# Gated linear attention followed by a gated state-space projection: weights loaded and converted by quarter, and the opening of the schedule put in another order

## The chip, the cores and the metric

The kernel runs on one core of one Trainium2 chip. The metric is device time in microseconds (us) of one execution; the number that counts is the median of several runs. Everything is float32 on the chip; the inputs q, k, v and alpha come as float32, the two weight matrices as float64, which the kernel converts itself.

## The reference, cut to what matters

```python
# q, k, v, alpha: (4 batches, 8 heads, 768 steps, 48)
for t in range(768):
    state = alpha[t][:, None] * state + outer(k[t], v[t])   # 48 x 48 for each batch and head
    y[t] = q[t] @ state
x = y with the heads side by side                            # (4, 768, 384)
val, gate = split(x @ w_in)                                  # w_in 384 x 1024, 512 each
for t in range(768):
    h = exp(A_log) * h + val[t]
    ys[t] = h
out = (silu(gate) * ys) @ w_out                              # w_out 512 x 384
```

## The kernel before, in words

**Blocks.** A block is 256 steps of one batch, so there are N = 12 blocks, three to a batch. Block m is worked in two halves. The attention half makes xT (the 384 features by 256 steps) from q, k, v and alpha. The projection half multiplies xT by `w_in` in four units of 128 inner channels (`project(n, cc)`, L882), runs the recurrence on VectorE, applies the gate and multiplies by `w_out` (`output`, L905).

**The attention half of block m.** The raw q, k, alpha lie by time in the partitions and have to be turned, so that the 48 features (two heads at 0 and 64) lie there. For the blocks 0 to 3 TensorE turns them by matmuls with an identity (`turned`, L677, the matmul on L682), each in two halves of eight time columns into two PSUM banks, and ScalarE copies them out (`copy_turned`, L688); `alphas` and `straighten` do this for alpha, and for q or k. For the later blocks VectorE's stream transpose does it (L592). A VectorE scan over alpha gives the running products P (`scan_P`, L627), a reversed one gives V (`scan_V`, L644), with three four-element steps between them (L636 to L642). `scaled_k` (L611) and `scaled_q` (L602) multiply k by V and q by P. TensorE makes the scores within chunks of 64 steps (`scores`, L720), VectorE masks them (`masks`, L730) while ScalarE copies the k columns beside them (L732), and TensorE multiplies them with v (`values`, L754; for block 0 `first_values`, L829). `states` (L781) makes the chunks' own states, VectorE adds them up (`add_banks`, L809; for block 0 `first_states`, L844 to L846), and `carried` (L767; `first_carried`, L837, for block 0) adds what earlier chunks bring. `join` moves the result into xT by small DMAs; for block 0 `first_join` does so by four ScalarE copies (L851 to L854).

**The weights.** Each is 64-bit, loaded as pairs of 32-bit words. `w_in` comes in two halves (`load_w`, two DMAs of 768 KB each), `w_out` in two. Six conversions (`low` and `convert`, units 0 to 3 for `w_in`, 4 and 5 for `w_out`) make float32: one ScalarE step (L541), two VectorE steps (L550, L552) and an integer add on GpSimd (L554).

**Turns.** The main loop runs over n. Turn n holds the projections of block n and the attention half of block n+1. What comes ahead of the loop is the attention half of block 0 and the scan of block 1. Turns 0 and 1 are written out by hand; from turn 2 on the body is regular.

**What sets the order.** The kernel runs in a manual schedule: each engine (TensorE or PE, VectorE or DVE, ScalarE or ACT, GpSimd or POOL) does its instructions in the order in which the program lists them, and waits by semaphores for what the others make. The DMAs are issued by SP in one order too (v of block 0 by POOL), each waiting for the eighth one before it to land. PSUM is eight banks: four that rotate (`mm`), two for scores and states (`s0`, `s1`) and two for y (`y0`, `y1`). A bank is taken when the work on its last contents is done.

These lines of turn 0 and turn 1 set the order of the work that the change touches:

```python
f0 = project(n, 0)                      # turn 0
copy_turned(tk, 1, turned(1, "k", 1, bank()))
tq = straighten(1, "q")
V = scan_V(1, P)
...
f3 = project(n, 3)
third(m)                                # end of turn 0's attention half
...
scores(m)                               # turn 1
alphas(3)
load_raw("a", 4, nc.sync)
convert(4)
masks(m)
```

Of the kernel before, what the change touches and what calls it, by code (L numbers as in the profile page):

```python
# [345 lines left out]
def fast(  # L346
# [99 lines left out]
    HW = NI // 2 * C  # L446
    wbits = [const.tile([C, NK, 2, HW, 2], U32, name=f"wbits{i}") for i in range(2)]
# [44 lines left out]
    def constants():  # L492
# [23 lines left out]
        for n, t in enumerate(Zqs):  # L516
# [4 lines left out]
            if n == 0:  # L521
                load_v(0, nc.gpsimd)
# [3 lines left out]
                for h in range(2):  # L526
                    nc.gpsimd.tensor_copy(out=mask[ds(L * h, L)], in_=tri[ds(L * h, L), ds(L * h, L)])

    def bits_of(i):
        if i < NI:  # L530
            t = wbits[i // 2].rearrange("p kk vg n two -> p (kk vg) n two")
            return t[:, :, ds(i % 2 * C, C), :], w_ins[i].rearrange("p kk vg n -> p (kk vg) n")
        return wobits[i - NI], w_outs[i - NI]
# [97 lines left out]
    def scan_V(m, P):  # L631
        al = als[m % 2]
        g = m % NG
        last = P[:, :, GC]
        if g:
            nc.vector.tensor_mul(ratio[:, m], last, ends[:, :, GC])  # L636
        else:
            nc.vector.tensor_scalar(out=ratio[:, m], in0=last, scalar1=1.0 / FIRST_PRODUCT, scalar2=None,
                                    op0=ALU.mult)
        nc.vector.reciprocal(ends[:, :, GC], last)  # L640
        if g < NG - 1:
            nc.vector.tensor_copy(out=lower[:, :, 0], in_=last)  # L642
# [3 lines left out]
                                     initial=0.0, op0=ALU.mult, op1=ALU.add)  # L646
        return by_place(V)
# [29 lines left out]
    def turned(m, name, part, t):  # L677
        raw = steps_of(name, m)
        tp = t.rearrange("p (j x) -> p j x", j=NJ // 2)
        for j in range(NJ // 2):  # L680
            for i in range(2):
                nc.tensor.matmul(tp[ds(64 * i, 64), j],  # L682
                                 raw[:, ds(i * ROW + (NJ // 2 * part + j) * D, 64)], ident,
# [3 lines left out]
    def copy_turned(to, part, tp):  # L687
        nc.scalar.activation(by_runs(to)[:, :, :, ds(NJ // 2 * part, NJ // 2)], tp, AF.Copy)  # L688

    def alphas(m, tag=None):  # L690
        to = by_place(als[m % 2])[:, :, 1:GP]
        for part, t in enumerate(bank_pair(tag)):
            copy_turned(to, part, turned(m, "a", part, t))

    def straighten(m, name):
        to = plain(name)
        for part, t in enumerate(bank_pair()):
            copy_turned(to, part, turned(m, name, part, t))
# [12 lines left out]
    def scores(m):  # L711
        Zk, Zq = Zks[m], Zqs[m % 2]
        scs[m] = [bank_pair("s"), bank_pair()]
        for c in range(G):
# [9 lines left out]
    def masks(m):  # L724
        sc = [[t[:, 0:4 * (L + D)].rearrange("p (h x) -> p h x", h=4) for t in pair] for pair in scs.pop(m)]
        mb = mask[:, None, :]
        if m < NG:
            for c in range(G):
                for i in range(2):
                    nc.vector.tensor_mul(As[i][:, c], sc[c][i][:, :, D:], mb.to_broadcast([C, 4, L]))  # L730
                for i in range(2):
                    nc.scalar.activation((K0, dS[m % 2][1])[i][:, c, :, 0:D], sc[c][i][:, :, 0:D], AF.Copy)  # L732
            return
# [98 lines left out]
    def first_carried(us):  # L832
        for u in us:
            for i in range(2):
# [47 lines left out]
    def project(n, cc):  # L882
# [7 lines left out]
        for vg, pj in enumerate((pv, pg)):  # L890
            for kk in range(NK):
                nc.tensor.matmul(pj, w_ins[cc][:, kk, vg, :], xT[:, kk, :],  # L892
                                 start=(kk == 0), stop=(kk == NK - 1))
        hh = p2.tile([C, GC], FP32, tag=f"h{cc}", name="hh")
        nc.vector.tensor_tensor_scan(  # L895
            out=hh, data0=a_dec[:, cc:cc + 1].to_broadcast([C, GC]), data1=pv,
            initial=prev_h[cc][:, GC - 1:GC] if n % NG else 0.0, op0=ALU.mult, op1=ALU.add)
# [266 lines left out]
```

## Time and profile before

| what | value |
|---|---|
| three runs | 287.44, 287.53 and 289.52 us, median 287.53 us |
| the profiled execution | 289.94 us, of which the span from the first to the last instruction is 288.1 us |
| TensorE clock that was granted | 0.998 |
| PE busy | 277.8 us, 96% of the span |
| DVE busy | 218.5 us, 76% |
| ACT busy | 110.3 us, 38% |
| POOL busy | 91.4 us, 32% |
| the chain that ended last | PE 91%, DVE 4%, ACT 1%, DMA 1% |
| in the first 70 us | PE busy 65.92 us, DVE 61.31 us |

Busy time is the union of an engine's instructions. A matmul's record is longer than the time that it keeps the next one waiting, so a PE that is busy throughout need not be at its peak; the time from one piece of the chain to the next says what a group of matmuls costs. Every matmul here has two records, so a projection unit of six matmuls is twelve. The first 55 us hold the part that the change touches; behind it PE hardly waits.

### The profile page before, as it was taken

Reading aid. Unit: us, or ns where it says so; the run is one execution under the profiler, and the core shown is the slowest. Engines: PE = TensorE matmul, PEld = TensorE weight load, DVE = VectorE, ACT = ScalarE, POOL = GpSimd, SP = SyncE. Lnnn points to the kernel's source line nnn. Section 1 sums busy time; section 2 is a strip of 40 time slices with the busy share of each in tenths; the row PEclk is TensorE's granted clock in tenths of the full one; section 3 lists DMA queues with packets and bytes.
Section 4 is the critical chain, followed back from the end, with each engine's and each line's share of the span. In section 5 each row is a group of like instructions: output and inputs, shape, how many; then the busy total and the mean of one; then the engine's idle time right before and its main releaser. Section 6 shows DMA issues by size and latency. Waiting matters only on the chain.

```text
span 288.1 us, 9591 instructions
## 1 busy us (share of the span) xinstructions
PE 277.8 (96%) x4096; PEld 221.0 (77%) x4096; DVE 218.5 (76%) x280; ACT 110.3 (38%) x242; POOL 91.4 (32%) x104
## 2 busy tenths in 40 slices
PE   7979999999999999999999999999999999999992
PEld 6968888886688688687688777787787786886860
DVE  7788999996599499499499498499498696289420
ACT  2664672642235335325325334333342451431110
POOL 8125220520046155152155164142163182142000
PEclk9999999999999999999999999999999999999999
DMA  6989753625591891991991971973872911101101
GB/s 186 345 250 351 243 144 69 146 56 134 151 229 33 209 224 35 222 208 36 217 213 45 258 160 48 261 155 73 226 164 65 266 40 35 57 16 30 55 6 63
DMA packets 51524, 41.22 MB, mean 143 GB/s; under 512 B 27312, under 2 KB 49264, under 8 KB 51472
## 3 DMA queue, kind: packets, MB, share of 16 engines
q1 hardware_dynamic: 50256, 39.37, 53.3%
q8 instruction: 34, 0.56, 0.9%
q10 hardware_dynamic: 960, 0.59, 0.8%
q0 software_dynamic: 256, 0.56, 0.7%
q14 instruction: 18, 0.15, 0.2%
HBM read 32.54 MB, written 4.72 MB: 129 GB/s over the span
## 4 chain that ended last, share of the span: by engine, by line
PE 91%; DVE 4%; ACT 1%; DMA 1%; issue 1%; DVEq 0%; ACTq 0%
PE mm L892 44%; PE mm L915 20%; PE mm L682 5%; PE y L767 4%; PE y L754 4%; PE s L781 4%; PE s L720 3%; PE mm L720 3%; PE mm L1129 2%; DMA raw_a<-in_alpha_dram 1%; PE s L682 1%; DVE V L644 1%; PE y L837 1%; PE y L829 1%; DVE hh L895 0%
## 5 line engine op out<-in xcount | busy, mean ns | idle before, releaser
L892 PE MATMUL mm<-xT,w_in 128*128 128x256 f32 x576 | 134.1, 385 | 0.6 <-issue 0.3
L892 PEld LDWEIGHTS mm<-xT,w_in 128*128 128x128 f32 x576 | 106.5, 190 | 17.8 <-issue 1.4
L915 PE MATMUL mm<-w_out,f_last 128*128 128x384 f32 x160 | 53.2, 486 | 0.0
L900 ACT ACTIVATE sg<-mm 128x256 f32<-128x256 f32 x48 | 18.4, 384 | 76.6 <-PE mm L892 76.4
L915 PEld LDWEIGHTS mm<-w_out,f_last 128*128 128x128 f32 x160 | 30.4, 190 | 19.1
L902 POOL TENSOR_TENSOR f_last<-sg,hh 128x256 f32<-128x256 f32 x36 | 27.2, 757 | 34.7 <-ACT sg L900 33.3
L801 POOL TENSOR_TENSOR sum<-sum,dS 128x192 f32<-128x192 f32 x30 | 30.1, 1003 | 19.9 <-ACT dS L789 18.4
L738 POOL TENSOR_TENSOR AK<-AK,mask 128x512 f32<-128x512 f32 x9 | 11.5, 1278 | 68.3 <-ACT AK L736 68.3
L895 DVE TENSOR_TENSOR_SCAN hh<-a_dec,hh,mm 128x256 f32<-128x256 f32 x32 | 23.0, 720 | 11.5 <-PE mm L892 10.6
L644 DVE TENSOR_TENSOR_SCAN V<-al,ends 128x1028 f32<-128x1028 f32 x12 | 30.5, 2545 | 0.1
L627 DVE TENSOR_TENSOR_SCAN P<-al,lower 128x1028 f32<-128x1028 f32 x12 | 28.4, 2368 | 2.5 <-ACT al L688 2.4
L909 ACT ACTIVATE o_sb<-mm 128x384 f32<-128x384 f32 x22 | 10.8, 490 | 46.1 <-PE mm L915 46.1
L735 DVE TENSOR_TENSOR A<-s,mask 128x256 f32<-128x256 f32 x9 | 3.8, 424 | 30.5 <-PE s L720 30.5
L592 DVE STREAM_TRANSPOSE k<-raw_k 128x1024 f32<-128x1024 f32 x9 | 18.3, 2028 | 0.0
L592 DVE STREAM_TRANSPOSE q<-raw_q 128x1024 f32<-128x1024 f32 x9 | 18.2, 2018 | 0.0
L602 DVE TENSOR_TENSOR Zq<-q,P 128x1024 f32<-128x1024 f32 (+1 forms) x14 | 16.3, 1166 | 0.3
L592 DVE STREAM_TRANSPOSE al<-raw_a 128x1024 f32<-128x1024 f32 x8 | 16.4, 2047 | 0.0
L554 POOL TENSOR_TENSOR w_in<-w_in,wr 128x768 int32<-128x768 int32 x4 | 9.2, 2289 | 22.5 <-DVE w_in L552 22.5
L754 PEld LDWEIGHTS y<-AK,v 64*64 64x64 f32 x352 | 12.2, 134 | 3.8 <-issue 3.3
L767 PEld LDWEIGHTS y<-Zq,sum 48*64 48x64 f32 x656 | 12.0, 134 | 4.0 <-POOL sum L801 2.7
L754 PE MATMUL y<-AK,v 64*64 64x64 f32 x352 | 14.7, 221 | 0.2 <-DVE lower L626 0.2
L611 DVE TENSOR_TENSOR Zk<-k,V 128x1024 f32<-128x1024 f32 (+1 forms) x14 | 14.7, 1051 | 0.2
(132 smaller groups left out, 378.4 us busy)
## 6 DMA issues: line engine op xcount, KB each, us to landing
out_dram<-o_sb SPq DMA_DIRECT2D x24, 192.0 KB, 3.2
v<-in_v_dram SPq DMA_DIRECT2D x22, 192.0 KB, 3.6
raw_k<-in_k_dram SPq DMA_DIRECT2D x18, 184.0 KB, 4.0
raw_q<-in_q_dram SPq DMA_DIRECT2D x18, 184.0 KB, 4.2
raw_k<-in_k_dram SPq DMA_DIRECT2D x18, 176.0 KB, 4.2
raw_q<-in_q_dram SPq DMA_DIRECT2D x18, 176.0 KB, 4.6
wbits<-in_moe_w_in_dram SPq DMA_DIRECT2D x4, 768.0 KB, 7.9
raw_a<-in_alpha_dram SPq DMA_DIRECT2D x16, 184.0 KB, 4.7
```

Of the source, the lines that this page charges most:

```text
L592: nc.vector.transpose(out=by_runs(to).rearrange("p h c j -> p h j c"), in_=raws[name][:, 0:4 * ROW].rearrange("p (h j d) -> p h j d", h=4, ...
L627: nc.vector.tensor_tensor_scan(out=P, data0=al[:, 0:4 * GP], data1=lower.rearrange("p h t -> p (h t)"), initial=0.0, op0=ALU.mult, op1=ALU ...
L644: nc.vector.tensor_tensor_scan(out=V[:, ::-1], data0=al[:, 1:4 * GP + 1][:, ::-1], data1=ends.rearrange("p h t -> p (h t)")[:, ::-1], init ...
L682: nc.tensor.matmul(tp[ds(64 * i, 64), j], raw[:, ds(i * ROW + (NJ // 2 * part + j) * D, 64)], ident, start=True, stop=True, skip_group_che ...
L754: nc.tensor.matmul(ys[m][i][ds(64 * s, 64), e, ds(c * C + h * L, L)], v_sb[rows, c, 4 * i + p, :], As[i][rows, c, p, :], start=across and ...
L767: nc.tensor.matmul(ys[m][i][ds(64 * s, 64), e, ds(u * L, L)], Ss[j][rows, p, :], Zqs[m % 2][rows, u, p, D:], start=False, stop=True, skip_ ...
L801: nc.gpsimd.tensor_add(Ss[j][:, :, 0:D], Ss[j - 1][:, :, 0:D], part)
L892: nc.tensor.matmul(pj, w_ins[cc][:, kk, vg, :], xT[:, kk, :], start=(kk == 0), stop=(kk == NK - 1))
L895: nc.vector.tensor_tensor_scan(out=hh, data0=a_dec[:, cc:cc + 1].to_broadcast([C, GC]), data1=pv, initial=prev_h[cc][:, GC - 1:GC] if n % ...
L900: nc.scalar.activation(sg, pg, AF.Silu)
L902: return lambda: engine.tensor_mul(fs[n][cc], sg, hh)
L915: nc.tensor.matmul(os[c], fs[n][cc][:, ds(c * C, C)], w_outs[cc // 2][:, cc % 2, :], start=(cc == 0), stop=(cc == NI - 1))
```

## The change

1. `w_in` is loaded by four units of 128 channels, two DMAs of 384 KB each, instead of two halves. Units 0 and 1 are issued ahead of block 1's q, as the first half was.
2. The loads that came next (alpha, k, q of block 2, v of block 1, units 2 and 3 of `w_in`, alpha of block 3) are issued later. A memset of one element of the raw alpha buffer on GpSimd (new L983), behind unit 1's integer add, has to be done before the first of them, and SP issues the others behind it. v of block 0 is loaded after GpSimd's other constants instead of between them.
3. Alpha of block 0 is turned in four quarters into four banks (`s0`, `s1`, `y1`, `y0`) instead of two halves.
4. `scan_V` is split: the steps that V does not need (block 0's ratio, and the copy of the last product) go to `after_V`, behind V or later.
5. All of k and q of block 1 is turned ahead of the loop: the second half of k between the two halves of block 0's scores, q behind block 0's states. VectorE's scans of block 1 are both ahead of projection unit 0's recurrence.
6. Unit 0's conversion stands between the two halves of block 0's masks, with its ScalarE step ahead of the masks' copies; unit 1's ahead of `first_states`.
7. `first_carried` runs by y bank instead of by chunk, and the very first projection unit runs by xT part (value and gate of part 0, then of part 1, then of part 2).
8. In turn 0 alpha of block 2 is turned ahead of the scores of block 1; alpha of block 3 is turned ahead of `third(1)`, where projection unit 3 was, and block 4's alpha is loaded there, ahead of `join`'s DMAs on SP. Unit 3 of block 0 goes to turn 1, between the scores and the masks of block 2; its recurrence goes behind the scan P of block 3, and its ScalarE step stays with the matmuls, ahead of the masks' copies. The gates' products of units 2 and 3 follow in turn 1, and both conversions of `w_out` stand behind unit 0 of block 1.

The core of the diff, with the ordering lines:

```diff
-    def load_w(half, engine):
+    def load_w(i, engine):
         for vg in range(2):
             engine.dma_start(
-                out=wbits[half][:, :, vg].rearrange("p kk n two -> p kk (n two)"),
+                out=wbits[i][:, :, vg].rearrange("p kk n two -> p kk (n two)"),
                 in_=moe_w_in.bitcast(U32).rearrange("(kk p) n -> p kk n", p=C)
-                [:, :, ds(2 * (vg * DI + HW * half), 2 * HW)])
+                [:, :, ds(2 * (vg * DI + C * i), 2 * C)])
...
+    def after_V(m, P):
         last = P[:, :, GC]
-        if g:
-            nc.vector.tensor_mul(ratio[:, m], last, ends[:, :, GC])
-        else:
+        if m % NG == 0:
             nc.vector.tensor_scalar(out=ratio[:, m], in0=last, scalar1=1.0 / FIRST_PRODUCT, scalar2=None,
                                     op0=ALU.mult)
+        if m % NG < NG - 1:
+            nc.vector.tensor_copy(out=lower[:, :, 0], in_=last)
...
     def first_carried(us):
-        for u in us:
-            for i in range(2):
+        for i in range(2):
+            for u in us:
...
-        for vg, pj in enumerate((pv, pg)):
-            for kk in range(NK):
-                nc.tensor.matmul(pj, w_ins[cc][:, kk, vg, :], xT[:, kk, :],
-                                 start=(kk == 0), stop=(kk == NK - 1))
+        order = [(vg, kk) for vg in range(2) for kk in range(NK)]
+        if n == 0 and cc == 0:
+            order.sort(key=lambda x: x[1])
+        for vg, kk in order:
+            nc.tensor.matmul((pv, pg)[vg], w_ins[cc][:, kk, vg, :], xT[:, kk, :],
+                             start=(kk == 0), stop=(kk == NK - 1))
...
     load_w(0, nc.sync)
+    load_w(1, nc.sync)
     load_steps("q", 1, [nc.sync])
...
-    alphas(0, "s")
+    alphas(0, ("s0", "s1", "y1", "y0"))
     tq = straighten(0, "q")
     tk = straighten(0, "k")
-    load_steps("a", 2, [nc.sync])
-    load_v(1, nc.sync)
-    load_w(1, nc.sync)
-    for name in "kq":
-        load_steps(name, 2, [nc.sync])
     alphas(1)
...
-    scores(0)
-    masks(0)
+    scores(0, [0])
+    copy_turned(tk, halves[1], turned(1, "k", halves[1], bank()))
+    scores(0, [1])
     low(0)
-    convert(0)
+    masks(0, between=lambda: convert(0))
+    after_V(0, P)
+    low(1)
     first_values(True)
-    first_states(states(0))
-    low(1)
+    st = states(0)
     convert(1)
+    first_states(st)
+    nc.gpsimd.memset(raws["a"][0:1, 0:1], 0.0)
+    load_steps("a", 2, [nc.sync])
+    load_w(2, nc.sync)
+    load_w(3, nc.sync)
+    for name in "kqa":
+        load_steps(name, 2 + (name == "a"), [nc.sync])
+    load_v(1, nc.sync)
     P = scan_P(1)
+    tq = straighten(1, "q")
     first_carried((1,))
...
         if n == 0:
+            V = scan_V(1, P)
             f0 = project(n, 0)
-            copy_turned(tk, 1, turned(1, "k", 1, bank()))
-            tq = straighten(1, "q")
-            V = scan_V(1, P)
+            scaled_k(1, tk, V)
+            scaled_q(1, tq, P)
             low(2)
-            scaled_k(1, tk, V)
+            f1 = project(n, 1)
             convert(2)
-            f1 = project(n, 1)
+            alphas(2)
             low(3)
-            scaled_q(1, tq, P)
+            first(m)
             f0()
             f1()
-            alphas(2)
             tk = straighten(2, "k")
...
             add_banks(m, st)
-            f3 = project(n, 3)
+            alphas(3)
+            load_raw("a", 4, nc.sync)
             third(m)
...
         elif n == 1:
             scores(m)
-            alphas(3)
-            load_raw("a", 4, nc.sync)
+            h3, f3 = project(0, 3, True)
+            masks(m)
+            f2()
+            P = scan_P(3)
+            h3()
+            values(m, True)
+            st = states(m)
+            add_banks(m, st)
+            f3()
+            f0 = project(n, 0)
             convert(4)
-            masks(m)
             junk(2)
             low(5)
-            values(m, True)
-            st = states(m)
-            P = scan_P(3)
-            f0 = project(n, 0)
-            add_banks(m, st)
             convert(5)
```

More of the change, by code (lines that the diff above doesn't have):

```diff
@@ L901, in project @@
         engine = nc.vector if n < 2 or n == N - 1 else nc.gpsimd
-        return lambda: engine.tensor_mul(fs[n][cc], sg, hh)
+        f = lambda: engine.tensor_mul(fs[n][cc], sg, hh)
+        return (scan, f) if late else f
     def output(n):
@@ L952, in fast @@
     P = scan_P(0)
-    V = scan_V(0, P)
-    half = turned(1, "k", 0, bank())
+    V = scan_V(0, P, False)
+    halves = [range(0, NJ // 2), range(NJ // 2, NJ)]
+    part = turned(1, "k", halves[0], bank())
     for c in range(G):
```

85 lines of the change are left out of this document (44 added, 41 removed).

## The prediction, as it was put on record

> **What bounds the kernel now.** I read the page first (PE busy 96%, 91% of the chain), then the chain in order of time, the table by windows, and the timelines of DVE, ACT and POOL up to 62 us. In the chain each piece runs to the start of the next:
>
> ```profile
> 24.69 3.00 PE mm L892 x12
> 27.69 2.77 PE mm L682 x48
> 30.46 2.79 PE mm L892 x12
> ...
> 53.32 0.46 PE y L754 x16
> 53.78 1.35 PE s L781 x48
> 55.13 5.38 PE mm L892 x24
> ```
>
> The second L682 piece (27.69) is the second half of block 1's k and all of its q: 2.77 us in the loop, while PE had idled ahead of it. From 55.13, block 1's first projection, to the end the chain is PE with under 1 us of gaps, so what counts is when PE gets there. The windows show the idle time (columns: PE, PEld, DVE, ACT, POOL busy, clock, DMA share, GB/s):
>
> ```profile
> 12.00:16.00 4.00, 3.10 (x70) 2.67 (x66) 3.90 (x5) 3.33 (x6) 0.00 (x0) 1.00 1.05 383
> 16.00:20.00 4.00, 3.63 (x144) 3.40 (x144) 2.99 (x7) 2.39 (x7) 0.36 (x1) 1.00 0.74 187
> 20.00:24.00 4.00, 3.13 (x116) 3.00 (x117) 3.63 (x6) 1.04 (x2) 2.45 (x2) 1.00 0.92 323
> ...
> 40.00:44.00 4.00, 4.00 (x75) 3.24 (x74) 3.76 (x5) 3.17 (x6) 0.00 (x0) 1.00 1.01 239
> ```
>
> PE is idle 0.90 + 0.37 + 0.87 = 2.14 us in 12 to 24 by the records, which overstate matmuls. DVE is as full as PE from 26 on, and its steps collide with POOL's adds (timelines of DVE and POOL):
>
> ```profile
> 22.78 2.29 DVE L627 TENSOR_TENSOR_SCAN P<-al,lower 128x1028 f32<-128x1028 f32 x1
> ...
> 33.03 2.55 DVE L602 TENSOR_TENSOR Zq<-q,P 128x1024 f32<-128x1024 f32 x1
> ```
> ```profile
> 23.01 3.68 POOL L554 TENSOR_TENSOR w_in<-w_in,wr 128x768 int32<-128x768 int32 x1 [1.55 <-DVE w_in L552]
> 32.66 1.84 POOL L554 TENSOR_TENSOR w_in<-w_in,wr 128x768 int32<-128x768 int32 x1 [5.98 <-DVE w_in L552]
> ```
>
> The add costs 1.82 alone (37.86) and 3.68 when a scan began before it; L602 costs 1.2 alone (74.05) and 2.55 when an add began before it. So a DVE step with two SBUF inputs and an add exclude each other. Masks (one input in PSUM) and stream transposes (one input) ran beside POOL unstretched (0.42 at 37.87, 2.04 at 79.85).
>
> **Ahead of the loop.** Quarters of alpha: the last ACT copy shrinks from 0.66 to about 0.43 (half of what exceeds the 0.20 of a tiny activation), so P starts at 8.30 instead of 8.53. Two small steps leave the path to V, but V still waits 0.22 for the reciprocal (42.79 to 43.01): 0.06 more. Block 0's scores start at 14.70 instead of 14.99 and take 1.0 for chunk pair 0. DVE by its row intervals: masks 15.81 to 16.48, unit 0's conversion (0.55 and 0.96) to 18.02, second masks to 18.68. PE: second half of k (0.95) to 16.65, second scores (0.80) to 17.45, 0.45 of `first_values`, a wait for the masks to 18.78. ACT, in order: the k copy to 17.35, L541 to 18.2 (0.92), four copies of 0.33 to 19.5, so `states` ends at 20.1 (19.88 before). Then q (1.85), 24 records of L837 (0.6), and the 98 records that took 2.43 at 21.71: 24.98. The first unit starts at once, since y bank 0 ends 0.6 earlier than bank 1 and the units go by part; before, PE stood 0.28 for xT. It costs 2.79 and ends at 27.8, against 27.69, and the 2.77 behind it are gone.
>
> **Weights and loads.** The pieces of `w_in` have rows of 1 KB instead of 2 KB. DMA engines full, 12 to 16 us moved 383 GB/s (rows of 1.5 and 2 KB), 40 to 44 us 239 GB/s (rows of 1.4 KB, strided). A unit of 0.79 MB costs 2.05 us by the first, 3.3 by the second. The two loads of the first half landed at 15.15 (7.45 + 7.7, tile view) and 17.2, q at 18.25. So unit 0 lands at 15.15 to 16.4 (needed 16.48), unit 1 at 17.2 to 19.6 (DVE 18.8, ACT 19.5: hidden), q at 18.25 to 20.7 against 20.1: 0 to +0.6. Rows of 1 KB are nearest to the 1.4 KB, but those go to 32 partitions each; I take 0.3. PE ends unit 0 at 28.1. The Trainium skill (DMA: Bandwidth & Descriptors, Specifications) puts the line rate at 512 B and above; by that rule the 0.3 would be 0, and the row of 239 GB/s does not bear it out for strided rows.
>
> v of block 0 is issued behind GpSimd's other constants, at about 6.0 instead of 3.1; it took 6.9 to land, so 13 to 14, needed at 17.45: nothing. SP stands behind the memset, that is behind unit 1's add, about 23.1. What is queued there: alpha 2 (0.39 MB), units 2 and 3, k, q 2, alpha 3, v 1, `w_out`, v 2. First landing 3.0 later (first row of the page's ACT issues), then 239 to 383 GB/s: alpha 2 by 26.5 to 27 (needed 30.9), unit 2 at 28.9 to 30.4, unit 3 at 31 to 33.7 (ACT needs it at 33.8), k at 32 to 35.3 (34.4), q at 33 to 37 (36.2), v 1 by 40 (42.2). ACT's L541 of unit 2 wants 28.5 and holds the next sigmoid and alpha's copies behind it; up to 31.5 it costs PE nothing. I take 0; bound 0 to +0.9 (k).
>
> **Turn 0 on DVE.** Unit 1's L550 (one SBUF input) at 18.8; its L552 (two inputs) waits for unit 0's add (18.21 to 20.03) and ends at 21.0; `first_states` to 22.1; unit 1's add 21.2 to 23.0 holds P to 23.0; P 25.3, V 25.6 to 27.9. Both scans are thus done when unit 0's values come at 27.65, so no chain of DVE stands ahead of the scores as V did before. Recurrence, L611, L602, recurrence, conversion: 33.05, ahead of block 1's scores (28.1 + 2.79 + 1.82 + 0.93 = 33.64). Masks 35.2, two gate products 35.9, P and V of block 2 to 40.75, conversion 42.25, recurrence 42.9, four sums 44.4, L611/L602 twice 45.65 and 46.85.
>
> **Turn 0 and 1 on PE.** 28.1 + unit 1 2.79 + turning alpha, k, q 5.5 + scores 1.70 + unit 2 2.79 + values and states 1.5 + alpha 3 1.87 + `third` 1.45 = 45.7. Scores of block 2: the second pair waits for 46.85 + 0.14: +0.3 (bounds 0 to 0.65). Unit 3 ends at 50.55. Values 0.62; the states need ACT's four copies, which now stand behind unit 3's sigmoid: 50.65, 0.35, then 0.21 to 0.33 each: the last at 52.0 to 52.3, states end at 52.6 instead of 52.09: +0.5. That is the change's own new wait: ACT holds K behind a step that waits for PE. What goes: before, PE took 2.46 for values and states there (52.67 to 55.13), 1.54 in regular turns: 0.92 of wait for the masks, which now have 2.8 us of unit 3 as cover. If that cover went, the 0.92 would be back.
>
> **The sum.** -2.77 (blocks turned in idle time) + 0.11 (unit 0's end) + 0.3 (q's landing) - 0.92 (wait for masks) + 0.3 (second scores) + 0.5 (K copies) = -2.5: block 1's projection at 52.6, not 55.13. Moved at nothing: units 2 and 3's gate products and the `w_out` conversions (covered by unit 0 and 1 of block 1; `output(0)` starts at 62.5, the last add ends near 60.2; before 61.86 and 64.85). DVE idles 2.41 at 69 and 3.12 at 75.6, enough for the 0.7 that it falls behind PE (masks of block 2 end 4.8 earlier, at 48.5, but 3.0 of steps moved behind them: -1.8 against -2.5). Against the profiled execution, 289.94 (288.1 and 1.84 around it): 287.4. The median shown is 2.41 lower: **285.0 us**.
>
> **Rivals.**
> - **L550 is held by the add too** (it takes 0.55 for 768 elements, L552 0.96). Conversion 1 ends at 21.55, V at 28.4, block 2's gate products come 0.3 later and the second scores wait 0.6: 285.3. For: no row shows L550 beside an add; against: transposes ran beside one. The Trainium skill (SBUF — State Buffer, Who interferes with whom) says that a tensor_scalar can enter a two-port mode that excludes GpSimd; the adds' rows agree with the exclusive lock, none shows it for L550.
> - **Nothing is late**: full-rate pieces, no wait of the second scores: -2.77 + 0.11 - 0.92 + 0.5 = -3.1: 284.4. For: 383 GB/s at 12 to 16.
> - **xT of block 1 comes late.** Alpha 4's four loads now stand ahead of `join`'s on SP. The xT pieces are issued 46.4 to 48.8; they took 2.0 to land at 49.8, up to 4.8 behind k's loads at 66: 50.8 to 53.6. At the latter +1.0: 286.0.
> - **The gain does not come**: the turned blocks only move the wait, because PE's idle time is broken by masks and copies. For: 2.14 of idle by records, less than 2.77; then 287.2 when copies and masks shift as much. Against: each piece has its wait (0.9 at 14, 0.6 at 21).
> - **Slower: the gate.** If unit 2 lands past 31.9, ACT and DVE stand, one for one. Even at 34.4, 1% slower at 37.3, 14 us behind the gate. The first half took 9.3 in a full queue: for; the queue is empty at the gate: against. 289.
>
> **How the numbers follow.** Forecast 0.40 (own range 284.6 to 285.6), L550 held 0.17, nothing late 0.20, xT late 0.12, no gain 0.06, gate 0.05. About 1% is what a measurement of this kernel can tell from no change: 284.65 and 290.4. Faster: 0.18 of nothing late, 0.07 of the forecast; slower: 0.04 of the gate. Range 284.1 to 287.3: it leaves out the gate and a quarter of nothing late.
>
> **What would show it.** Right: q turned between the states and the first carried products, at 20 to 22, the first unit near 25, no turning of k or q between units 0 and 1, block 1's projection near 52.6, ACT's K copies behind a sigmoid at 51. Wrong: SP's rows of wbits past 32, PE waiting for DMA at q or xT, or waits for the DVE scans.

## The result, and the profile after

The changed kernel takes 291.56 us (median of 9 runs, 290.68 to 294.38); the kernel before takes 288.26 us beside it (9 runs, 287.44 to 290.98). The ratio is 1.0115, with a 95% interval of 1.0082 to 1.0148: slower by 1.15%. The forecast was 285.0 us, with a range up to 287.3, so the sign was wrong. Of the 6.6 us to the forecast, 0.73 is its base: it started from a median of 287.53 us over three runs, and nine gave 288.26. Ratios and intervals, here and below, are formed from executions in the chip's faster state alone (for e1 this leaves out 291.17 and 291.24) and are not the quotient of the medians shown. The profiled execution of the changed kernel took 291.37 us (span 289.7).

The chain of the changed kernel, in order of time (start, duration, what), shows that the front half went as planned and where it broke:

```profile
25.61 5.38 PE mm L901 x24
...
46.95 0.99 SPq L409
...
49.50 6.40 DMA xT<-yst
55.90 0.14 issue
56.04 7.11 PE mm L901 x24
```

Units 0 and 1 now stand together (25.61, 24 matmuls in 5.38) and nothing is turned between them. But block 1's projection starts at 56.04, not at 52.6, and what stands ahead of it is no longer PE or DVE: the chain runs through SP's queue (L409, the load of raw alpha) into the small DMAs that make xT. The waits of PE in the first 70 us (us in total, times, longest) say the same:

```profile
PE mm L901 <- DMA xT<-yst: 3.1, 1, 3.1
```

SP's timeline of the changed kernel (start, duration of the issuing, what) shows what was in front of them:

```profile
23.28 1.18 SPq L420 DMA_DIRECT2D raw_a<-in_alpha_dram  x2
...
38.53 5.70 SPq L409 DMA_DIRECT2D raw_k<-in_k_dram  x4
44.33 1.80 SPq L409 DMA_DIRECT2D raw_q<-in_q_dram  x4
46.23 3.18 SPq L409 DMA_DIRECT2D raw_a<-in_alpha_dram  x4
49.50 2.79 SPq L881 DMA_DIRECT2D xT<-yst  x4
```

Three groups of block-size loads, 1.2 MB, are issued from 38.5 to 49.4, and SP's four xT pieces come behind the third. The pieces took up to 6.7 us to land. POOL issues the other four pieces, at 47.0 to 48.5 and behind nothing of SP's queue; they took as long (5.1 to 6.7). So it is not only the order on SP's queue that holds them, but also what the DMA engines still have to move. And the wait cost more than its own 3.06 us. The windows around it (length, busy PE, PEld, DVE, ACT, POOL, granted clock, DMA share, GB/s):

```profile
53.00:56.00 3.00, 0.00 (x0) 0.00 (x0) 1.40 (x4) 0.00 (x0) 0.00 (x0) 1.00 0.94 185
56.00:58.00 2.00, 1.96 (x8) 1.65 (x9) 0.19 (x1) 0.00 (x0) 0.00 (x0) 0.81 0.21 42
58.00:60.00 2.00, 2.00 (x6) 1.65 (x5) 1.97 (x4) 0.00 (x0) 0.00 (x0) 0.50 0.00 0
```

PE does nothing in the first row while DMA is full; then the granted clock is 0.50, by its own records for 3.41 us from 57.24 on, and the two units take 7.11 instead of 5.38: another 1.73. The Trainium skill (TensorE: Matmul & The Clock Gate, Part 1) says that an idle window of about 3.4 us halves the clock and that about as much work gives it back; this trace agrees in the length of the slow stretch (3.41), but the wait ahead of it, 3.06, was shorter than that window.

### The profile page after: what moved, and what is told of

Its sections match the earlier page's. It is cut to its first block, busy times and chain, and to the rows that moved or that the text cites. A ratio compares the mean times of both kernels' runs of the same rounds, so it can differ in the third digit from the quotient of the medians.

```text
span 289.7 us, 9607 instructions
## 1 busy us (share of the span) xinstructions
PE 277.7 (96%) x4096; PEld 221.5 (76%) x4096; DVE 220.7 (76%) x280; ACT 110.6 (38%) x244; POOL 95.3 (33%) x105
## 4 chain that ended last, share of the span: by engine, by line
PE 91%; DVE 3%; DMA 2%; SPq 1%; issue 1%; ACT 1%; DVEq 0%; ACTq 0%
PE mm L901 45%; PE mm L930 20%; PE y L761 4%; PE y L774 4%; PE s L725 4%; PE s L788 4%; PE mm L685 3%; PE mm L725 3%; DMA xT<-yst 2%; PE mm L1150 2%; PE y L709 1%; PE y L844 1%; SPq L409 1%; DVE V L645 1%; DVE P L626 1%
## 5 line engine op out<-in xcount | busy, mean ns | idle before, releaser
L901 PEld LDWEIGHTS mm<-xT,w_in 128*128 128x128 f32 x576 | 107.8, 192 | 20.8 <-issue 4.0
L916 POOL TENSOR_TENSOR f_last<-sg,hh 128x256 f32<-128x256 f32 x36 | 32.9, 915 | 28.1 <-ACT sg L914 26.5
L645 DVE TENSOR_TENSOR_SCAN V<-al,ends 128x1028 f32<-128x1028 f32 x12 | 29.9, 2493 | 0.4
L553 POOL TENSOR_TENSOR w_in<-w_in,wr 128x768 int32<-128x768 int32 x4 | 7.3, 1828 | 29.1 <-DVE w_in L551 19.2
L601 DVE TENSOR_TENSOR Zq<-q,P 128x1024 f32<-128x1024 f32 (+1 forms) x14 | 15.0, 1070 | 0.3
L761 PE MATMUL y<-A,v 64*64 64x64 f32 x352 | 14.5, 221 | 0.0
```

The source lines that it names most:

```text
L601: nc.vector.tensor_mul(Zqs[m % 2][:, ds(u0, n), :, D:].rearrange("p u h t -> p h u t"), t[:, :, at].rearrange("p h (u t) -> p h u t", t=L) ...
L645: nc.vector.tensor_tensor_scan(out=V[:, ::-1], data0=al[:, 1:4 * GP + 1][:, ::-1], data1=ends.rearrange("p h t -> p (h t)")[:, ::-1], init ...
L761: nc.tensor.matmul(ys[m][i][ds(64 * s, 64), e, ds(c * C + h * L, L)], v_sb[rows, c, 4 * i + p, :], As[i][rows, c, p, :], start=across and ...
L901: nc.tensor.matmul((pv, pg)[vg], w_ins[cc][:, kk, vg, :], xT[:, kk, :], start=(kk == 0), stop=(kk == NK - 1))
L916: f = lambda: engine.tensor_mul(fs[n][cc], sg, hh)
```

## The experiments

Each ran beside the kernel before on one chip; e1 to e4, e5 to e8, e9 to e11, and e12 with e13 ran on four different chips, on which the median of the kernel before was 288.03 to 288.44 us. "k 3", "q 3" and "alpha 4" are the loads of block 3's raw k and q and of block 4's raw alpha. "The exchange" is a part of the change's last point: unit 3 of block 0 goes to turn 1, and the turning of alpha 3 and the load of alpha 4 take its place. "K copies" are the four ScalarE steps (L737) that copy block 2's k columns for its states. One thing has to be taken out before traces are compared: in each execution TensorE's full clock began at another time (4.3 to 7.6 us), and with it the first scan P of block 0 (at 7.0 to 8.8). So the table gives, for the profiled execution of each kernel, that start, the first projection unit, the projection of block 1, and how far this lies behind P. "Stalls" are PE's waits over 0.15 us for nothing that the profile shows ("issue"), up to 60 us.

| kernel | median us | ratio, 95% interval | P(0) | unit 0 | block 1's projection | behind P(0) | stalls | half clock |
|---|---|---|---|---|---|---|---|---|
| before | 288.26 | 1 | 8.53 | 24.69 | 55.13 | 46.60 | 0.58 | 0 |
| changed | 291.56 | 1.0115 [1.0082, 1.0148] | 7.83 | 25.61 | 56.04 | 48.21 | 0 | 3.41 |
| e1 alpha 4 behind xT | 288.28 | 1.0018 [0.9986, 1.0050] | 7.44 | 25.42 | 52.98 | 45.54 | 0 | 0 |
| e2 no gate | 291.06 | 1.0105 [1.0072, 1.0138] | 8.37 | 28.11 | 57.36 | 48.99 | 3.36 | 0 |
| e3 no gate, alpha 4 behind | 291.57 | 1.0109 [1.0068, 1.0149] | 7.86 | 27.71 | 56.14 | 48.28 | 2.88 | 0 |
| e4 filler ahead of block 1's projection | 291.18 | 1.0098 [1.0064, 1.0132] | 7.59 | 25.37 | 56.54 | 48.95 | 0.88 | 0 |
| e5 k 3, q 3, alpha 4 behind xT | 287.46 | 0.9965 [0.9935, 0.9994] | 7.36 | 25.14 | 52.38 | 45.02 | 0 | 0 |
| e6 e5, K copies first | 286.88 | 0.9948 [0.9921, 0.9976] | 8.30 | 26.08 | 52.79 | 44.49 | 0 | 0 |
| e7 exchange undone | 289.60 | 1.0026 [0.9995, 1.0057] | 7.32 | 25.37 | 55.67 | 48.35 | 0.90 | 0 |
| e8 before + exchange | 289.96 | 1.0051 [1.0020, 1.0081] | 7.47 | 23.18 | 54.48 | 47.01 | 0.52 | 0 |
| e9 before + k, q turned first | 292.18 | 1.0150 [1.0107, 1.0192] | 7.99 | 27.91 | 57.91 | 49.92 | 1.99 | 6.83 |
| e10 e6 + 0.79 MB ahead of the gate | 286.82 | 0.9940 [0.9911, 0.9969] | 7.29 | 25.50 | 52.22 | 44.93 | 0 | 0 |
| e11 e8, loads behind, copies first | 288.21 | 1.0005 [0.9979, 1.0030] | 8.84 | 24.14 | 54.14 | 45.30 | 0 | 0 |
| e12 e9 + gate | 289.30 | 1.0047 [1.0015, 1.0078] | 7.23 | 25.30 | 55.21 | 47.98 | 0 | 0 |
| e13 e6 + 2.36 MB ahead of the gate | 289.86 | 1.0045 [1.0008, 1.0081] | 6.98 | 28.55 | 55.26 | 48.28 | 2.03 | 3.41 |

The half clock at the end of each span, where PE has run out of work, is left out.

### e1 to e4: which wait, and what it costs

Theory A: alpha 4's loads ahead of xT on SP. B: the gate packs the loads together. C: the clock that halves after a wait.

```diff
 # e1: alpha 4 behind the xT pieces
             alphas(3)
-            load_raw("a", 4, nc.sync)
             third(m)
+            load_raw("a", 4, nc.sync)
 # e2: no gate
-    nc.gpsimd.memset(raws["a"][0:1, 0:1], 0.0)
 # e3: both edits
 # e4: six matmuls into a bank pair ahead of project(1, 0)
+            for t in bank_pair():
+                for _ in range(3):
+                    nc.tensor.matmul(t[:, 0:256], wide_S[0][:, 0:C], wide_S[0][:, 0:256], start=True, stop=True,
+                                     skip_group_check=True)
```

> The changed kernel with one move: the four loads of block 4's alpha are issued behind the xT pieces of block 1 instead of ahead of them. Theory A (the order on SP's queue): in the changed kernel the four xT pieces of SP were issued at 49.5 because alpha's four loads stood ahead of them until 49.4, and they landed at 55.9 behind alpha's data; alone they can be issued near 47 and land near 52.5, just behind q of block 3 (its last piece landed at 51.8). Then block 1's projection starts at 53.0 to 53.5 instead of 56.04, the TensorE clock stays at full speed, and the span is about 285.0 us, ratio to the kernel before 0.988 to 0.992. Theory B (the held-back loads as a whole, not this order): k and q of block 3 still fill the queue, the xT pieces land at 54 to 55, PE waits 1 to 2 us, ratio 0.995 to 1.002.

> The changed kernel without the one-element memset that holds the loads back; block 4's alpha stays ahead of the xT pieces. Theory B: the loads of block 2 start at about 11 instead of 23.3, k and q of block 3 have landed by about 46 to 47 as in the kernel before, alpha of block 4 lands near 50 and the xT pieces near 51 to 52, so block 1's projection starts near 53, ratio to the kernel before about 0.99. Theory A: alpha's four loads still keep SP until 47 to 49, and xT lands at 53 to 55 with a wait of up to 2 us, ratio 0.995 to 1.005. If the loads hurt the opening when they are not held back, the first projection unit starts later than 25.6.

> The changed kernel without the memset that holds the loads back and with block 4's alpha issued behind the xT pieces of block 1. Theories A and B agree: nothing stands ahead of the xT pieces, they land near 49 to 50, block 1's projection starts near 53.0, held only by the K copies behind unit 3's sigmoid, full clock throughout, span near 285.0, ratio 0.987 to 0.991. If PE still waits there for a DMA, both are wrong.

> The changed kernel with six idle matmuls (2.8 us of PE work on a constant tile, result unused) ahead of block 1's projection, where PE waited 3.06 us for xT. Theory C (the wait itself halves the clock afterwards): xT still lands near 56, but the two projection units take 5.4 us instead of 7.11, the clock stays at full speed, and the kernel is about 1.7 us faster than the changed one, ratio to the kernel before about 1.005. Rival: the units were slow for another reason (xT pieces one by one, banks, weights): they take about 7 us again and the ratio stays near 1.0115.

**e1** took the loss away (1.0018) and missed the gain that theory A promised (0.988 to 0.992). In its profile the projection follows at once behind the second scores, unit 3 and the states. That is 0.4 us from the 52.6 that the prediction gave, but this is luck, since P(0) came early; measured from P it is 45.54 against 44.3:

```profile
51.62 1.35 PE s L788 x48
52.98 5.51 PE mm L901 x24
```

That profiled execution, 286.35 us, was the best of twelve, though; others went up to 290.51. The tile view of xT suggests why. The line gives shortest, median and longest time from issue to landing; first the changed kernel's last pieces, then e1's:

```profile
DMA to landing us min/median/max: 4.7/5.7/6.7
```
```profile
DMA to landing us min/median/max: 5.0/5.1/5.6
```

The pieces still took 5 us behind k 3 and q 3. Issued from 46.5 on, the last landed at 53.8, when PE was already in the first unit. There was no margin; that xT was late in the slower executions is not shown, since only one has a profile.

**e4** shows theory C by itself. With six matmuls that nobody reads in the gap, the clock stays whole and the two units take 5.18 instead of 7.11:

```profile
53.75 2.79 PE mm L1069 x12
56.54 5.18 PE mm L901 x24
```

The filler ends at 56.54, later than PE went on in the changed kernel (56.04), and the execution had a stall of 0.88 in unit 3, so the median gains next to nothing (291.18; a ratio of about 1.005 was expected, 1.0098 came).

**e2 and e3** went against A and B alike: without the gate the kernel is as slow as with it, and moving alpha 4 no longer helps. PE does not wait for xT there either. The waits of PE in e2:

```profile
PE mm L685 <- issue: 1.5, 1, 1.5
...
PE y L761 <- issue: 1.2, 1, 1.2
...
PE mm L901 <- issue: 0.7, 1, 0.7
```

"Issue" means that nothing the profile records held the engine. A new theory, D, came from the trace's DMA packets. 34 of them, of 16,384 bytes each, fit PE's code:

```profile
q8 instruction: 34, 0.56, 0.9%
```

(queue and kind, packets, MB, share of the 16 engines; the line is the same in before and after.) Counting all of PE's records, that is matmuls, weight loads and the waits of its sequencer, every one of the 22 stalls over 0.15 us in the traces of before, after and e1 to e9 ends at a record whose number (from 0) is 193 or 194 modulo 256, that is at one place of a 256-record block, and 1.2 to 1.6 us after one of these packets had landed. So PE had run to the end of a block whose successor was not there yet. Without their stalls, e2 and e3 would stand 45.6 and 45.4 behind P(0), where e1 stands (45.54). How long a block is in coming can be measured from the moment at which PE enters the block before it: the packet started 0.3 to 0.8 us later where DMA was nearly idle (the changed kernel and e5, packets that start at 16 to 26 us), and 2.1 to 5.2 us later where it was full (before and e2, packets that start at 19 to 33 us).

The Trainium skill (Runtime: NRT & Kernel Launch, Instruction fetch mechanics) describes blocks of 16 KiB, 256 instructions, that the sequencer fetches in order by a DMA queue of its own while it executes the block before, and calls the cost mostly hidden. The size and the order agree with these traces; that it is hidden does not hold here where the data queues are full (stalls of 0.5 to 2.0 us).

### e5 to e8: the loads, ACT's order, and the exchange by itself

```diff
 # e5: no loads of k 3 and q 3 behind the turning; behind xT instead
             third(m)
+            load_raw("k", 3, nc.sync)
+            load_raw("q", 3, nc.sync)
+            load_raw("a", 4, nc.sync)
             load_v(3, nc.sync)
 # e6: e5, and in project(n, cc, late=True) the sigmoid is issued with the scan, behind the K copies
 # e7: exchange undone (turn 0, then turn 1)
-            alphas(3)
-            load_raw("a", 4, nc.sync)
+            f3 = project(n, 3)
             third(m)
...
             scores(m)
-            h3, f3 = project(0, 3, True)
+            alphas(3)
+            load_raw("a", 4, nc.sync)
             masks(m)
 # e8: the kernel before, with the exchange alone
```

> The changed kernel with three groups of loads (raw k 3, raw q 3, alpha 4) all issued on SP behind the xT pieces of block 1, not only alpha 4. Theory A (the bytes that are in flight when the xT pieces are issued decide; the spread of the run with alpha 4 alone behind, 286.35 to 291.24, is k 3 and q 3 still in flight in some executions): xT lands 2 to 3 us after its issue, block 1's projection starts at 53.0 without a wait for DMA, the granted clock stays whole, the executions draw together near the best of that run: median 286.4 to 287, ratio 0.992 to 0.996. Rival D (late fetches of instruction code make the spread, and they are late whatever is loaded): projection at 53.0 in some executions, with stalls of PE for nothing shown in others, median stays 288.3, ratio 1.00, spread of 4 us or more.

> As the run with the three groups of loads behind, and in addition ACT issues the sigmoid of unit 3 of block 0 behind the four K copies of block 2 (its multiply and scan follow as before). Theory A with the prediction's term of +0.5 for the K copies: the copies end near 48.5, the states near 52.2, projection at 52.1 to 52.4, 0.6 to 0.9 us less than the run with the loads behind alone: ratio 0.989 to 0.993. Rival (the copies were not what the states waited for, or xT lands only at 53): no difference from that run.

> The changed kernel with the exchange undone: unit 3 of block 0 is projected in turn 0 again, alpha 3 turned and alpha 4 loaded in turn 1 behind the scores of block 2, as before the change; the units of w_in, the gate and the order of q and k stay. Theory A (the whole loss is alpha 4 ahead of xT; the rest of the change gains what the prediction said): no wait for DMA, the 0.92 of wait for the masks is back and the 0.5 of the K copies gone, projection of block 1 at 53.2 to 53.8, ratio 0.993 to 0.997. Rival D (loads that stand closer together behind the gate delay code and weights whatever the exchange): PE stalls for nothing shown or for DMA elsewhere between 25 and 55, projection at 55 or later, ratio 1.00 to 1.01.

> The kernel before with the exchange alone: in turn 0 alpha 3 is turned and alpha 4 loaded in the place of unit 3, which is projected in turn 1 between the scores and the masks of block 2. Theory A: alpha 4 goes ahead of the xT pieces here too, PE waits 2 to 3 us for xT ahead of block 1's projection, the granted clock falls to half after it, projection at 56.5 to 57.5, ratio 1.005 to 1.012. Rival (the loads of before are spread wider, so xT is in time): the masks' 0.92 goes and 0.5 to 0.8 come for the second scores and the K copies, projection at 54.7 to 55.1, ratio 0.998 to 1.000.

**e5** is faster than the kernel before (0.9965), though by less than expected. xT now comes 1.9 to 3.8 us after issue (tile view of e5), and the executions spread over 286.0 to 289.7 instead of e1's 286.4 to 290.5:

```profile
DMA to landing us min/median/max: 1.9/2.9/3.8
```

So A is right once all three groups are counted: the bytes in flight when xT is issued decide, not alpha 4 alone.

**e6** gains a further 0.53 us behind P(0) (45.02 to 44.49), the size of the prediction's term of +0.5. From its unit 3 on, the chain of e6 no longer has ACT in it:

```profile
51.26 0.62 PE y L761 x32
51.89 0.91 PE s L788 x48
52.79 5.38 PE mm L901 x24
```

The interval of its ratio overlaps that of e5, and neither reached the 0.989 to 0.993 expected of e6, so it is the traces and not the medians that show this step: from the first unit to block 1's projection e5 takes 27.24, and e6, e10 and e13, which all have the copies first, take 26.71, 26.72 and 26.71.

**e7** missed: no DMA wait, but not the gain either. PE waited 1.9 us for unit 3 itself:

```profile
PE mm L901 <- POOL w_in L553: 1.9, 1, 1.9
...
PE mm L685 <- issue: 0.9, 1, 0.9
```

The add of unit 3 began at 42.36, since the change had put its conversion behind the scans of block 2, and without the exchange PE is ready for the unit at 42.3, not at 48. The exchange and the late unit belong together. e7 so does not isolate the exchange, but it shows that the rest of the change, as it stands, can't do without it.

**e8** is slower than before (1.0051), but its profile shows no wait for xT (3.0 to 4.5 us to land, the last 1.2 us ahead of PE), only a stall of 0.52 and a first scan that took 0.37 longer: it began at 7.47, while POOL's copies of the constants (L519, 6.30 to 7.99) were still running. Neither theory had both the time and the place right; e11 goes on from it.

### e9 to e11: the other part by itself, and bytes that should hurt

```diff
 # e9: the kernel before, k and q of block 1 turned first
     scores(0)
+    copy_turned(tk, 1, turned(1, "k", 1, bank()))
     masks(0)
...
     P = scan_P(1)
+    tq = straighten(1, "q")
     first_carried((1,))
...
-            f0 = project(n, 0)
-            copy_turned(tk, 1, turned(1, "k", 1, bank()))
-            tq = straighten(1, "q")
             V = scan_V(1, P)
+            f0 = project(n, 0)
 # e10: e6, half of w_out ahead of the gate
     load_steps("q", 1, [nc.sync])
+    load_w_out(0, nc.sync)
 # e11: e8 with the loads of e5 and the ACT order of e6
```

> The kernel before with one part alone: the second half of block 1's k is turned behind the scores of block 0, all of its q behind the states, and V of block 1 is scanned ahead of unit 0's scan; the halves of w_in, the loads and the exchange stay as before. Theory A (the 2.77 of the sum is the true gain): the turning of k and q goes from between units 0 and 1, the first unit starts 0.9 to 1.3 later, at 25.6 to 26.0, the scores of block 1 are reached about 1.6 us earlier (35.3 instead of 36.9), the projection of block 1 at 53.3 to 53.8, ratio 0.993 to 0.996. Rival (DVE is the bound there, 26.43 to 35.58 without a gap, so that PE's time only moves into a wait ahead of the scores): ratio 0.998 to 1.002.

> The best version so far (loads behind, K copies first) with the first half of w_out, 0.79 MB that nothing waits for before 55 us, loaded ahead of the gate, behind q of block 1, so that DMA has work at 17 to 21 us, where it stood still. Theory D (code of PE is fetched by the same 16 DMA engines as data and comes late behind it): the fetch that began at 17.6 comes 2 to 3 us later, PE stands 0.6 to 1.7 us for nothing shown at 20 to 23, the first unit is as much later, median 0.5 to 1.7 us more than the best version: ratio 0.997 to 1.001. Rival (the stalls without the gate came from the loads being in the way of something else, or are chance): no stall there, median the same or less, since fewer bytes are left for 30 to 40 us: ratio 0.993 to 0.996.

> The kernel before with the exchange alone, but with raw k 3, raw q 3 and alpha 4 loaded behind the xT pieces, and the K copies of block 2 ahead of unit 3's sigmoid. Theory A (what the exchange alone lost, 1.5 us by its median, is xT late in most executions): the loss goes, the masks' wait is gained, ratio 0.994 to 0.998. Rival (it lost elsewhere: fetches of code, or DVE's order in turn 1): ratio 1.002 to 1.006 as without the change of loads.

**e9** was the greatest surprise: the part that carried 2.77 of the sum is, alone, the slowest kernel of all (1.0150). Turning q at 20 to 22 us in the kernel before, where the loads run without a gate, takes PE to the end of a block of code early and makes it wait for the next; the chain of e9:

```profile
24.02 0.63 PE y L837 x22
24.65 1.99 issue
...
27.91 8.12 PE mm L892 x24
```

The block in question was asked for at 20.28 at the earliest, when PE entered the block before; its packet started at 24.20, landed at 25.08, and PE went on at 26.64. The clock then fell to half for 6.83 us, and the two units took 8.12 instead of 5.38.

**e10** missed on D's side: no loss against e6. Its trace shows that it was no test of the block that counts: 0.79 MB at some 390 GB/s were through by 18, the packet asked for at 16.17 started 1.70 later (0.46 in e5), and PE stood only 0.12. e13 does it with more.

**e11** removes e8's loss (1.0005 against 1.0051; the intervals just overlap). The loss goes, as A said, but A's gain (0.994 to 0.998) does not come. The profiled projection does stand 1.30 us earlier behind P(0) than before's, but 0.86 of this was there already at the first unit (15.30 behind P against 16.16), up to which the two programs are the same: there before's execution had its stall of 0.58. From the first unit on the exchange is worth 0.44 in this trace (30.00 against 30.44), which is too little for the medians to show.

### e12 and e13: bytes taken away from a stall, and bytes put where there is none

```diff
 # e12: e9, and a gate ahead of the loads that fill DMA at 20 to 24
     first_states(states(0))
+    nc.vector.memset(raws["a"][0:1, 0:1], 0.0)
+    load_steps("a", 2, [nc.sync])
+    load_w(1, nc.sync)
+    for name in "kq":
+        load_steps(name, 2, [nc.sync])
+    load_v(1, nc.sync)
 # e13: e6, with loads that nothing waits for ahead of the gate
     load_steps("q", 1, [nc.sync])
+    for half in range(2):
+        load_w_out(half, nc.sync)
+    for m in (1, 2):
+        load_v(m, nc.sync)
```

> The kernel before with k and q of block 1 turned first (the run that was 1.5% slower, with a stall of 1.99 us at 24.65 and half the clock after it), and a gate in front of the loads of alpha 2, the second half of w_in, k 2, q 2 and v 1: DVE writes one element of alpha's buffer behind the first states, near 22. Theory D (the block of code that starts at record 961 was asked for at 20.3 and fetched only 3.9 later, behind 10 us of queued loads): the fetch starts within 1 us of the crossing, no stall of PE at 24 to 27, no half clock, and the turning's gain shows: first unit at 25.0 to 26.2, projection of block 1 at 53.0 to 54.0, ratio 0.992 to 0.998. Rival (the stall comes from the order of PE's code, not from loads): the stall stays over 1 us, ratio 1.010 or more; or the second half of w_in, now landing near 31, holds DVE: ratio 1.000 to 1.006.

> The best version (loads behind, K copies first) with both halves of w_out and v of blocks 1 and 2, 2.36 MB that nothing waits for before 40 us, loaded ahead of the gate behind q of block 1. The run with 0.79 MB there had its last byte near 18, and showed the fetch at 1.70 behind the crossing instead of 0.5. Theory D: the bytes now flow from 16 to 23, the fetch that is asked for at 16.2 starts 2.5 to 4 later, PE stands 0.7 to 2 us for nothing shown near 20 to 22, all that follows is as much later: ratio 0.997 to 1.002. Rival (fetches go by their own way and the stalls without the gate came of something else): no stall over 0.3, ratio 0.992 to 0.996.

These two settle D. In **e13** DMA is busy from 16 to 22, where e6 has it nearly empty (0.23 of it busy from 16 to 18, then less). Windows of e6, then of e13:

```profile
18.00:20.00 2.00, 1.65 (x78) 1.51 (x73) 2.00 (x4) 1.88 (x6) 1.67 (x1) 1.00 0.00 0
20.00:22.00 2.00, 2.00 (x63) 1.95 (x57) 1.94 (x5) 0.64 (x2) 0.30 (x2) 1.00 0.03 8
```
```profile
18.00:20.00 2.00, 1.78 (x81) 1.59 (x76) 1.97 (x4) 0.89 (x2) 0.83 (x1) 1.00 1.04 395
20.00:22.00 2.00, 0.19 (x3) 0.18 (x4) 1.93 (x5) 0.00 (x0) 1.47 (x1) 0.84 1.03 248
22.00:24.00 2.00, 2.00 (x21) 2.00 (x20) 2.00 (x1) 0.60 (x1) 0.36 (x2) 0.50 0.45 89
```

The packet that is asked for at 15.87 starts 3.60 later (0.46 in e5), lands at 20.57, and PE, which ran dry at 19.78, goes on at 21.81: a stall of 2.03 out of nothing but loads that nobody waits for, and the clock halves again behind it. Its median is 2.98 us above e6's (on another chip; by the two ratios 2.8), and its ratio of 1.0045 is more than the 0.997 to 1.002 expected.

**e12** is the reverse. The gate brings the packet that was 3.91 late in e9 down to 0.40, the 1.99 of stall and the slow clock are gone, and 2.9 us of e9's median with them (292.18 to 289.30; by the two ratios 3.0). The rest of the expectation missed: it is still slower than before. The chain of e12 shows the bound that the simple count of PE's work overlooks:

```profile
30.89 1.92 PE mm L682 x32
32.81 0.68 DVE hh L895
33.49 2.45 DVE Zq L602
...
35.99 1.00 PE s L720 x32
```

PE is early, and then waits for DVE's recurrence and the q product ahead of block 1's scores. Turning first pays only where DVE has been put in a new order too, as the change did; this trace shows the bound. Against before, the first unit stands 1.91 later behind P(0) (18.07 against 16.16), 0.61 of it because the first scan ran into POOL's copies as in e8 (2.91 instead of 2.30), and only 0.53 is won back from there to block 1's projection.

The best of the runs, e6 and e10, beat the kernel before by 0.5 to 0.6% and the changed kernel by about 1.6%, worked out from the medians (286.88 and 286.82 against 291.56).

## Why the prediction was wrong

Its own steps, in order:

- **Ahead of the loop.** P of block 0 came at 7.83 instead of 8.30, since the clock came at 6.04 (in e6, with the same opening and the clock at 6.93, P came at 8.30); measured from P, block 0's scores stand where they were forecast (6.40 behind P, 14.70 less 8.30). From there to the first unit the sum was too short: 25.61 is 17.78 behind P, against 17.0 forecast (25.3 less 8.3). The states ended 12.33 behind P instead of 11.8, and the first carried products and values took 3.56 instead of 3.03 (0.6 and 2.43). So the 2.77 of turning was only partly hidden, in part as the rival "the gain does not come" had it: against before, the first unit stands 1.62 later behind P (17.78 against 16.16), where 0.84 was forecast. The smaller parts of the change (quarters of alpha, the order by bank and by part) were not run by themselves.
- **Weights and loads.** q's +0.3 was nothing: q landed at 17.99, before it was wanted at 20.16. ACT stood for unit 2 of `w_in` until 30.6, inside the 31.5 that the prediction allowed, and PE did not; the gate rival did not come about. The list of what is queued behind the gate ended with v 2, however. Raw k 3 and raw q 3 on the same queue between there and xT were not carried on, and alpha 4 came in only as a rival; in the sum, xT's landing behind these 1.2 MB stood at nothing. **That is the step that failed.** In its place the runs showed a wait of 3.06 us, which goes when the three groups are issued behind xT (e5). The prediction's own signs of being wrong named a wait for DMA at xT.
- **Turn 0 and 1 on PE.** 27.3 us were forecast from the first unit to block 1's projection. e5, where the loads do not interfere, took 27.24. The masks' wait is gone as forecast, and the K copies behind the sigmoid cost the +0.5 that was put down for them (0.53 between e5 and e6).
- **Rival "xT of block 1 comes late"** named the place, and was priced at most 1.0 us from the 4.8 that xT once took behind k's loads. It cost 3.06 of wait and 1.73 of half clock. The price had SP's last piece issued at 48.8, and it was issued at 51.8, since alpha 4's loads kept SP until 49.4; and it went by one group of loads ahead, where the pieces stood behind three and took up to 6.7. That a wait of 3 us has a second price was nowhere in the sum.
- **The sum.** Forecast for block 1's projection, measured from P: 52.6 - 8.30 = 44.3. Found: 48.21, that is 3.91 more, of which 3.06 is the wait and about 0.8 the first unit. With the 1.73 behind it, and P 0.70 earlier, the scores of block 3 should stand 48.21 - 46.60 + 1.73 - 0.70 = 2.64 later than before. They do (80.40 against 77.76). Without the 0.70 the loss is 3.34, close to the 3.30 of the medians. The two profiled executions end closer together (291.37 against 289.94): before's was 1.68 above its median, and lost 0.88 against the other between block 3's scores and 261 us, in the regular part.
- **L550 held by the add** did not happen in the changed kernel, where no such step began beside an add. But the mechanism exists: in e9 (lines below, DVE and POOL) L550 began 0.52 us before an add's end and took 0.93 instead of 0.55, and in e12 0.94. So steps with one SBUF input are held too, not only those with two:

```profile
21.47 0.93 DVE L550 TENSOR_SCALAR w_in<-wbits 128x768 uint32<-128x768 uint32 x1
```
```profile
20.16 1.82 POOL L554 TENSOR_TENSOR w_in<-w_in,wr 128x768 int32<-128x768 int32 x1 [12.15 <-ACT wr L541]
```

What the prediction left out altogether is D. The gate, which it weighed as the rival that could lose, is what keeps DMA free at 18 to 23 us for PE's code. Without it (e2) the kernel is as slow as with the fault in xT; with it and the loads behind xT (e5, e6) the change gains 1.0 to 1.6 us by the medians, where 2.5 were forecast for the change and 3.0 with the K copies first.

What stays open is the spread of the executions: e5 and e6 still range over 2 to 4 us. Stalls at code blocks appear in some traces and not in others near 130 and 172 us too, 0.2 to 0.8 each, in the regular part that no edit touched, and might account for part of it; only one execution of each kernel has a profile.

## What to carry to other kernels

When a load is moved on a queue, follow the queue past the moved piece to the next transfer that PE will wait for, and count every byte that will be in flight at that moment. A PE that waits 2 to 3 us may pay twice, since in three of these traces its clock halved behind such a wait. And leave DMA some air where PE runs through small matmuls quickly: here its code came in blocks of 256 instructions and came late when the DMA engines were full of data, and waits that the profile puts down to "issue" were the sign of it.

## What the runs showed of the hardware that was not expected

- **Code blocks.** A 16-KB packet itself took 0.88 to 1.6 us beside idle DMA engines and 0.88 to 1.8 beside full ones (packets of all fifteen traces), and where PE stalled it went on 1.2 to 1.6 us after the landing. What full queues change is the start: the packet that mattered in e9 started 3.9 us after it could have been asked for.
- **The clock can halve after 2 us.** A stall of 1.99 (e9) and one of 2.03 (e13) were followed by 6.83 and 3.41 us of half clock; ones of 1.47 (e2) and 1.71 (e3) were not. Counted from the moment at which the full clock first came, the halvings began 17.07 (e13), 20.48 (e9) and 51.20 us (the changed kernel) later, that is 5, 6 and 15 times 3.413. How long PE stood within the stretch of 3.41 us does not decide it alone: 1.60 in e13's was followed by half the clock, 1.71 in e3's was not. What does stays open.
- **Four elements can take 1.6 us.** In the changed kernel's timelines of DVE and of POOL, the ratio step of four elements starts beside an add and ends with it; alone it takes 0.17. In all ten kernels here with this order it took 1.45 to 1.60 and ended within 0.03 us of the add. The scan of block 1, which begins 1.0 before the end of the next add, takes 3.15 instead of 2.30.

```profile
18.13 1.60 DVE L633 TENSOR_SCALAR ratio<-P 128x4 f32<-128x4 f32 x1
```
```profile
17.88 1.82 POOL L553 TENSOR_TENSOR w_in<-w_in,wr 128x768 int32<-128x768 int32 x1 [9.85 <-DVE A L735]
```
